# A hand-kept list scheduler gets a new order of loads, a later end and a longer wait for hosts

## The chip, the cores and the metric

One Trainium2 chip, one core of it. The kernel is one launch. Its time is the device time of that core in microseconds; lower is better. The matrix engine is TensorE (PE; its weight loads are listed as PEld), VectorE is DVE, ScalarE is ACT, GpSimd is POOL, and SyncE (SP) issues most of the transfers.

## The reference

Two branches share one normalized input. The first is a diagonal state-space layer (S4D) over 2048 tokens and 576 channels, which the reference does as a long convolution with a kernel of sums of 128 complex exponentials; the second is a two-layer perceptron with 4608 hidden units. Everything is float32.

```python
x = A_u                                   # 1 x 2048 x 576
xn = _layernorm(x)
# branch A: K[d, l] = 2 Re sum_n C[d, n] exp(A[d, n] dt[d] l), y = causal convolution of xn with K
dt = jnp.exp(log_dt)
A = -jnp.exp(log_A_real) + 1j * A_imag    # 576 x 128 poles
C = (C_real + 1j * C_imag) * dt[:, None]
P = jnp.exp((A * dt[:, None])[:, :, None] * pos[None, None, :])
K = 2.0 * jnp.einsum("dn,dnl->dl", C, P).real
y = irfft(rfft(u, 2L) * rfft(K, 2L))[:L] + u * D_skip
# branch B
g = silu(gelu(_layernorm(xn) @ w1 + b1) @ w2 + b2)
out = x + y * g
```

## The kernel before

**The perceptron is the frame.** Its products run in 48 slots. A slot takes three blocks of 128 hidden units (G = 3) and 512 tokens (TB). First come three *hidden blocks*, 14 matmuls of 512 columns each (`layer1`, L546), each followed by GELU on ACT (L578), a rounded copy `hh` on ACT (L581) and the remainder `hl = h - hh` on DVE (L584): float32 is done as sums of products of such pairs. Then comes the second layer: a transposed part for the last 128 channels (L630) and four groups of nine matmuls of 448 columns, one group for each 128 tokens (L638). After each group DVE adds the result to `acc` (L643). Four slots are "turned" and do the second layer in halves of 288 columns instead (L608, added at L615). The results of hidden blocks and of groups take turns in two PSUM banks, m0 and m1, so a new block can start only when the one two before it in the row has been read: the first hidden block of a slot needs the add of the third group of the slot before.

**The weights** arrive as `raw`, and are split the same way into a rounded part (ACT, L530) and a remainder (DVE, L527). The second layer's tile is laid out in one of two ways. A *joined* set keeps all 576 columns of a row together and is split in three pieces of 576; any other keeps 448 and 128 columns apart and is split in pieces of 448, 384 and 896. `JOINED` (L456) lists the joined sets; a set serves two slots as a rule.

**The state-space branch is fitted in between.** Before it can start, the poles' *polar form* (`params`, from L778) must be worked out: four arrays, log_A_real (buffer `kt`), C_real (`pr`), C_imag (`mg`) and A_imag (`kt` again), are each loaded by four transfers of SP in pieces of 128 bytes (L793) and turned by DVE (L800); then come square roots, arctangents and sines on ACT, and on DVE reciprocals (L820, L832) and products. A table for each 16 channels follows (`tables`), and from each table a product on PE (`kgen`, L981) that makes a piece of the convolution kernel. The convolution itself is done on PE in small tiles for chunks of 96 channels (`chunk`: L1053, L1092, L1145, and the last inverse step L1177), six chunks in all; each ends with a store to `s_s` in device memory. A group of these small matmuls between two matmuls of the frame is called a *visit* below. A table's product can `ride` in a visit of the convolution, its *host*, or make a visit alone.

**Tokens 512 to 2047 are normalized** by statistics on DVE (L383, L385), roots on ACT (L389), a reciprocal and a scaling on DVE (L393, L405); the inputs are loaded by SP (L358). Tokens of the second half go back to memory for later (`y_s`, L407).

**The order is made at build time.** `Order` is a list scheduler: *lines* of steps, each step with an engine, a planned duration, needs, and perhaps an earliest time (`at`). At each point it takes, of the lines' next steps, the one that can start earliest; between equals the line that stands first in `od.lines`. What it traces is then fixed: each engine runs its instructions in that order, and an instruction that waits holds back everything behind it on its engine. A load is a step without an engine, and its planned duration is only a guess of when the data are there:

```python
fetch = [step(None, 6.0, lambda k=k: load(k), at=t, mark=("praw", k)) for k, t in ((0, 44.0), (2, 56.0), (3, 60.0), (1, 66.0))]
```

The line `nl` holds the norms, `pl` the polar form. At the end, `ml` holds the last stores: for the last 96 channels of tokens of the first half it loads the convolution's result (L706, into `xc`), multiplies it by the gate (`gated`, L711) and adds the input (`summed`, L716). `END` (L1535) is the planned time by which the convolution's steps are spread out, and `ALONE` (L1536) is how long a table's product that is ready waits for a host before it goes alone.

Of the kernel before, what the change touches and what calls it, by code (L numbers as in the profile page):

```python
# [23 lines left out]
NCH = D // CH  # L24
# [19 lines left out]
def dve(n):  # L44
    return 0.075 + 0.00104 * n
# [163 lines left out]
def step(eng, dur, fn, need=(), mark=None, cv=0, at=0.0, late=0.0, tbl=None, by=1e9):  # L209
    return dict(eng=eng, dur=dur, fn=fn, need=tuple(need), mark=mark, cv=cv, at=at, late=late, tbl=tbl, by=by)  # L210
# [3 lines left out]
def mixer_kernel(ctx, tc, u, log_a_real, a_imag, c_real, c_imag, log_dt, d_skip, w1, b1, w2, b2,  # L214
# [19 lines left out]
    def dram(ap_of, offset, ap):  # L234
        return bass.AP(tensor=ap_of.tensor, offset=ap_of.offset + offset, ap=ap)
# [217 lines left out]
    SEQ = [(n, g, tb) for n, (g, tbs) in enumerate(SETS) for tb in tbs]  # L453
    FIRST, GATE = (0, 3, 2 * NG, 2 * NG + 1), (2 * NG - 4, 2 * NG - 1)
    TURNED = (2 * NG - 4, 2 * NG - 1, 4 * NG - 2, 4 * NG - 1)
    JOINED = {SEQ[slot][0] for slot in TURNED} | set(range(6))  # L456
    DT = D - DA
    for n, (g, _) in enumerate(SETS):
        PARTS += [(n, g, 1, i) for i in range(KB + 1)] + [(n, g, 2, i) for i in range(G)]
# [37 lines left out]
    def split_raw(low_on=nc.vector):  # L497
# [14 lines left out]
        else:  # L512
            joined, m = half in JOINED, P
            if i == 0:
# [178 lines left out]
    def combine_load(b, n, c0, c1, part=None):  # L693
        m = c1 - c0
        if part is None:
            XS[b] = [sb.tile([P, D], F32, name="row", bufs=NROW)[:, :n * m].rearrange("p (i d) -> p i d", i=n) for _ in range(3)]
        elif part == 0:
            kt = [sb.tile([P, 12, 64], F32, name="kt", bufs=2).rearrange("p a b -> p (a b)") for _ in range(2)]
            xc = sb.tile([P, 2, 32, 24], F32, name="xc", bufs=NXC).rearrange("p a b c -> p (a b c)")
            XS[b] = [t[:, :n * m].rearrange("p (i d) -> p i d", i=n) for t in (kt[0], xc, kt[1])]  # L700
        x, s, g = XS[b]
        if part != 1:
            nc.gpsimd.dma_start(x, u_s[:, b:b + n, c0:c1])
            nc.gpsimd.dma_start(g, g_s[b:b + n, :, c0:c1].rearrange("i p d -> p i d"))
        if part != 0:
            nc.gpsimd.dma_start(s, s_s[:, b:b + n, c0:c1])  # L706
# [71 lines left out]
    def params():  # L778
# [12 lines left out]
        def load(k):  # L791
            for q in range(4):
                nc.sync.dma_start(PRM[k][32 * q:32 * q + 32, :D].rearrange("p (b j) -> p b j", j=32), dram(  # L793
                    src[k], 32 * q, [[N, 32], [32 * N, D // 32], [1, 32]]))
        fetch = [step(None, 6.0, lambda k=k: load(k), at=t, mark=("praw", k)) for k, t in ((0, 44.0), (2, 56.0), (3, 60.0), (1, 66.0))]
        add(None, 12.0, lambda: nc.sync.dma_start(dt, dram(log_dt, 0, [[0, P], [1, D]])), at=24.0)
        add("ACT", act(D), lambda: nc.scalar.activation(dt, dt, AF.Exp), tbl="exp", late=0.0)
        V, A = nc.vector, nc.scalar
# [16 lines left out]
        t = T[2]  # L815
# [396 lines left out]
    od = Order(tc, nc)  # L1212
    od.pinned = True
    el, wl2, wl, nl2, pl, pl2, pl3, pl4, pl5, nl, ml, ml2, xl, wx, c3, c2, c1, kl, tl, sl, vl, gl, fl, f2l = [od.line() for _ in range(24)]
# [117 lines left out]
    def row_lines():  # L1332

        Y = [A2F[:, k:k + TB] for k in (2 * D, PT0 + 4 * D, 0, D, PT0 + 4 * D + TB, PT0 + 4 * D + 2 * TB)]
        X, T = [Y[k] for k in (0, 1, 2, 0, 3)], Y[4:]

        def store(t):
            nc.gpsimd.dma_start(dram(y4_s, t * P * D, [[D, 64], [64 * D, 2], [1, D]]), YT[4 + t])

        def load(i):  # L1340
            for q in range(4 if i < KB else 2):
                y = X[i][32 * q:32 * q + 32]
                if i < KB:
                    nc.gpsimd.dma_start(y.rearrange("p (b d) -> p b d", b=4), dram(
                        y4_s, i * P * D + P * q, [[D, 32], [32 * D, 4], [1, P]]))
                else:
                    nc.gpsimd.dma_start(y.rearrange("p (b j) -> p b j", j=32), dram(
                        y4_s, KB * P + 32 * q, [[D, 32], [32 * D, NT], [1, 32]]))

        def blocks(i):  # L1350
            x, y = T[i % 2], X[i]
            if i < KB:
                nc.vector.transpose(x.rearrange("p (k b t) -> p k b t", k=4, b=4),
                                    y.rearrange("p (b k j) -> p k b j", k=4, b=4))
            else:
                nc.vector.transpose(x[:64], y[:64])

        def places(i):
            y = T[i % 2]
            c = slice(i * P, (i + 1) * P)  # L1360
            if i < KB:
                return y.rearrange("p (k t) -> p k t", k=4), XH[:, :, 1, c], XL[:, :, 1, c]
            return y[:64], XR[:64, 1], XR[64:, 1]

        def high(i):
            y, h, _ = places(i)
            nc.scalar.activation(h, y, AF.Copy)

        def low(i):
            y, h, lo = places(i)  # L1370
            nc.vector.tensor_sub(lo, y, h.bitcast(F32))
        issue = od.line()
        for i in range(KB + 1):
            out = od.line()["steps"]
            if i < KB:
                out.append(step("POOL", 0.7, lambda i=i: store(i), need=[("yn", 4 + i)], mark=("yo", i)))
            out.append(step(None, 6.0, lambda: None, need=[("yo", min(i, 3))], mark=("ys", i)))
            issue["steps"].append(step("POOL", 2.4 if i < KB else 1.2, lambda i=i: load(i), mark=("yi", i),
                                       need=[("ys", i)] + ([("yt", 0)] if i == 3 else [])))
            od.line()["steps"].append(step(None, 5.0 if i < KB else 7.0, lambda: None, need=[("yi", i)], mark=("yl", i)))  # L1380
            a, b, c = od.line(), od.line(), od.line()
            a["steps"].append(step("DVE", dve(TB), lambda i=i: blocks(i), mark=("yt", i),
                                   need=[("yl", i)] + ([("y2", i - 2)] if i > 1 else [])))
            b["steps"].append(step("ACT", act(TB), lambda i=i: high(i), mark=("yh", i), need=[("yt", i)]))
            c["steps"].append(step("DVE", dve(TB), lambda i=i: low(i), need=[("yh", i)], mark=("y2", i) if i < KB else ("x", 1)))
        k = [i for i, x in enumerate(od.lines) if x is pl][0]
        od.lines = od.lines[-26:] + od.lines[:k] + [nl] + [x for x in od.lines[k:-26] if x is not nl]

    YB = []

# [43 lines left out]
    def weigh_in(which):  # L1434
# [3 lines left out]
        end = od.t["PE"] + sum(ln[G:] if which == 1 else ln[:G])  # L1438
        apart = which == 2 and SEQ[turn[0]][0] not in JOINED
        for i in range(m):  # L1440
# [27 lines left out]
    def w2_parts(n, j, hid):  # L1468
        if n in JOINED:
            return hid  # L1470
# [22 lines left out]
    for k in range(4):  # L1493
        gl["steps"].append(step("POOL", 5.0, lambda k=k: part.update({k: load_g2(k)}), mark=("g2", k),
                                need=[("g2c", k - 1)] if k else []))
# [24 lines left out]
    def end_line():  # L1520
        for c, c0, c1, sets in ((NCH - 3, 0, CE, [(b, 1) for b in range(8)]), (NCH - 2, CE, CL, [(0, 4), (4, 4)])):
            for b, n in sets:
                a = (b, n, c0, c1)
                ml["steps"].append(step(None, 8.0 if b else 12.0, lambda a=a: combine_load(*a), need=[("st", c), ("u", NT - 1)]))
                ml["steps"].append(step("DVE", 2 * dve(n * (c1 - c0)), lambda a=a: (gated(*a), summed(*a))))
                ml["steps"].append(step(None, 4.0, lambda: None))
        a = (0, 8, CL, D)
        ml["steps"].append(step(None, 1.0, lambda: combine_load(*a, 0), need=[("k1", NCH - 1, 1), ("x1", NCH - 1)]))
        ml["steps"].append(step(None, 11.0, lambda: combine_load(*a, 1), need=[("st", NCH - 1)]))
        ml["steps"].append(step("DVE", dve(8 * CH) + 0.1, lambda: gated(*a)))  # L1530
        ml["steps"].append(step("DVE", dve(8 * CH) + 0.1, lambda: summed(*a)))


    pace = dict(left=NCH * (2 + 2 + 4), last=0.0, started=False)
    END = 930.0  # L1535
    ALONE = 5.0  # L1536

    def pe_turns(limit=1, any_time=False, all_lines=True):
        for x in (nl, pl, ml) + ((c3, c1, kl) if all_lines else ()):
            n = 0  # L1540
            while n < (2 if x in (c1, nl) else limit):
# [3 lines left out]
                if x is c1:  # L1545
                    now = od.t["PE"]
                    gap = (END - now) / max(pace["left"], 1)
                    if n == 0 and pace["started"] and now < pace["last"] + 0.50 * gap and not any_time:
# [20 lines left out]
    later(mid - 4, G - 1, lambda: x_free(0))  # L1569
    later(mid - 1, G - 1, lambda: x_free(1))  # L1570
    later(NSLOT - 10, 4, end_line)
    sl["steps"].append(step(None, 11.0, last_s, need=[("st", NCH - 1)], mark="s8"))
    for k in range(8):
        c3["steps"].append(step(None, 5.0 if k == 0 else 2.0, lambda k=k: last_x(k), need=[("i1", NCH - 1), ("u", NT - 1)], mark=("x8", k)))

# [49 lines left out]
    for slot in range(NSLOT):  # L1625
# [4 lines left out]
        for pos in range(NPOS):  # L1630
            if pos < G:
                need = wmark(n, 1) + [("x", tb)]
# [16 lines left out]
                for k, (a, b, c) in enumerate(cell, pos + 1 - len(cell)):  # L1649
                    by = hidden_by(pos, k)  # L1650
                    if slot == NSLOT - 1 and k:
                        a = seeded(a, tb, k)
# [6 lines left out]
            else:  # L1659
# [6 lines left out]
                need = [wmark(n, 2)[i] for i in w2_parts(n, j, hid)] + [("h", slot, i) for i in hid]  # L1666
# [19 lines left out]
                if last or halves:  # L1686
                    add = cell[0]
                    dh, k = (terms[0][1], 1) if halves else (0, 2)
# [9 lines left out]
                    if final:  # L1698
                        b = 8 + 4 * tb + j
                        x, y = (el, el2) if slot < NSLOT - 1 else (od.line(),) * 2  # L1700
# [72 lines left out]
```

## Time and profile before

| | |
|---|---|
| median of three runs | 1068.91 us (1068.3 to 1071.31) |
| the profiled execution | 1070.33 us, its span 1068.2 us |
| PE busy | 1057.6 us, 99% of the span |
| DVE busy | 936.7 us, 88% |
| ACT busy | 677.4 us, 63% |
| granted TensorE clock | 0.999 |

The span runs from the first to the last instruction; 2.1 us of the execution's time lie outside it. Matmuls overlap, and their ends are modelled, so what a matmul costs is read from start to start: an undisturbed one of 512 columns is listed with 0.39 us and is followed by the next after 0.227 us.

### The profile page before, as it was taken

The numbers are of one execution on the slowest core, as the hardware profiler recorded it, in microseconds if no ns is written. First come the engines' busy times: TensorE is split into PE (matmuls) and PEld (weight loads), VectorE is DVE, ScalarE is ACT, GpSimd is POOL, SyncE is SP. The second block draws the span as 40 slices with busy tenths as digits, with TensorE's granted clock in tenths as the row PEclk, the third lists the DMA queues.
The fourth block names the chain that finished last, engine by engine and source line by source line (L and its number), as shares of the span: only waits on it lengthen the run. The fifth ranks groups of instructions, "written<-read, shape, count | busy, mean of one in ns | idle before, by whom it ended". The sixth has DMA issues, their size and how long they took to land. (4 is left out here: it accounts for less than half of the span.)

```text
span 1068.2 us, 23535 instructions
## 1 busy us (share of the span) xinstructions
PE 1057.6 (99%) x9515; PEld 874.5 (82%) x9515; DVE 936.7 (88%) x1550; ACT 677.4 (63%) x1056; POOL 212.2 (20%) x294
## 2 busy tenths in 40 slices
PE   9999999999999999999999999999999999999997
PEld 7887888888878887888878888788877888778886
DVE  7688768889999899999999999899899999957656
ACT  6567639877655767657667675666685675625344
POOL 5668743201000002000120000200002022322020
PEclk9999999999999999999999999999999999999999
DMA  7885446664223143454521315222421446465145
GB/s 230 238 259 171 121 144 224 214 163 142 62 69 91 43 100 99 120 134 116 124 83 48 110 39 121 74 75 64 96 86 45 132 118 150 125 188 162 24 126 170
DMA packets 149213, 130.93 MB, mean 123 GB/s; under 512 B 99020, under 2 KB 121072, under 8 KB 148080
## 3 DMA queue, kind: packets, MB, share of 16 engines
q1 hardware_dynamic: 132592, 79.76, 28.2%
q0 software_dynamic: 15760, 48.70, 14.9%
q8 instruction: 75, 1.23, 0.5%
q10 hardware_dynamic: 752, 0.97, 0.3%
q14 instruction: 34, 0.28, 0.1%
HBM read 98.90 MB, written 35.19 MB: 126 GB/s over the span
## 5 line engine op out<-in xcount | busy, mean ns | idle before, releaser
L638 PE MATMUL m<-w2s,hh 128*128 128x448 f32 x1056 | 301.9, 367 | 0.4 <-DVE acc L643 0.2
L638 PEld LDWEIGHTS m<-w2s,hh 128*128 128x128 f32 x1056 | 196.1, 188 | 28.9 <-issue 7.0
L578 ACT ACTIVATE h<-m,b1t 128x512 f32<-128x512 f32 x144 | 99.2, 689 | 188.2 <-PE m L546 183.6
L638 PE MATMUL m<-w2s,hl 128*128 128x448 f32 x528 | 191.5, 363 | 0.0
L546 PE MATMUL m<-XH,w1h 128*128 128x512 f32 x564 | 155.5, 398 | 0.0
L546 PE MATMUL m<-XL,w1h 128*128 128x512 f32 x564 | 151.6, 391 | 0.0
L546 PE MATMUL m<-XH,w1l 128*128 128x512 f32 x564 | 151.0, 390 | 0.0
L584 DVE TENSOR_TENSOR hl<-h,hh 128x512 fp32r<-128x512 f32 x144 | 99.1, 689 | 53.7 <-ACT hh L581 53.3
L546 PEld LDWEIGHTS m<-XH,w1h 128*128 128x128 f32 x564 | 103.4, 188 | 30.9 <-issue 9.1
L546 PEld LDWEIGHTS m<-XL,w1h 128*128 128x128 f32 x564 | 105.9, 188 | 23.0
L546 PEld LDWEIGHTS m<-XH,w1l 128*128 128x128 f32 x564 | 105.9, 188 | 22.4
L881 POOL DMA_DIRECT2D par<-par_s x36 | 27.4, 762 | 484.2 <-DVE mg L924 423.7
L643 DVE TENSOR_TENSOR acc<-m,acc 128x448 f32<-128x448 f32 x160 | 98.4, 615 | 19.0 <-PE m L638 17.7
L638 PEld LDWEIGHTS m<-w2s,hl 128*128 128x128 f32 x528 | 99.1, 188 | 7.4
L630 PE MATMUL m<-hh,w2s 128*128 128x512 f32 x264 | 98.9, 402 | 0.0
L581 ACT ACTIVATE hh<-h 128x512 fp32r<-128x512 f32 x144 | 90.6, 630 | 3.3
L530 ACT ACTIVATE w2s<-raw 128x576 fp32r<-128x576 f32 (+3 forms) x75 | 46.4, 675 | 48.6 <-PE m L638 47.0
L924 DVE TENSOR_TENSOR mg<-par 128x1024 f32<-128x1024 f32 x72 | 67.9, 952 | 0.7
L630 PEld LDWEIGHTS m<-hh,w2s 128*128 128x128 f32 x264 | 49.6, 188 | 17.5 <-issue 5.1
L527 DVE TENSOR_TENSOR w1l<-raw,w1h 128x384 fp32r<-128x384 f32 x98 | 49.8, 558 | 13.8 <-ACT w1h L530 13.7
L546 PE MATMUL m<-XR,w1r 128*128 128x512 f32 x141 | 54.9, 389 | 0.0
L546 PE MATMUL m<-XR,w1s 128*128 128x512 f32 x141 | 54.9, 389 | 0.0
(227 smaller groups left out, 1866.3 us busy)
## 6 DMA issues: line engine op xcount, KB each, us to landing
raw<-in_B_w_dram SPq DMA_DIRECT2D x75, 288.0 KB, 3.5
raw<-in_B_w_dram SPq DMA_DIRECT2D x100, 192.0 KB, 3.4
par_s<-A POOLq DMA_DIRECT2D x8, 1080.0 KB, 5.6
par<-par_s POOLq DMA_DIRECT2D x36, 240.0 KB, 3.4
f2t<-f2q SPq DMA_DIRECT2D x24, 256.0 KB, 3.8
raw<-in_B_w_dram SPq DMA_DIRECT2D x50, 96.0 KB, 3.9
u_s<-in_A_u_dram POOLq DMA_DIRECT2D x16, 288.0 KB, 4.1
xc<-xn_s SPq DMA_DIRECT2D x48, 96.0 KB, 4.1
```

The lines of the kernel that those rows point to most:

```text
L527: low_on.tensor_sub(lo, r[:m], h[:m].bitcast(F32))
L530: nc.scalar.activation(h, r, AF.Copy)
L546: nc.tensor.matmul(q, a, b, start=j == 0, stop=j == len(ops) - 1)
L578: nc.scalar.activation(t, q, AF.Gelu_apprx_tanh, bias=b1t[:, g * G + i:g * G + i + 1], scale=1.0)
L581: LAST[0] = nc.scalar.activation(hh[:, i], t, AF.Copy)
L584: nc.vector.tensor_sub(hl[:, i], t, hh[:, i].bitcast(F32))
L630: nc.tensor.matmul(q, a[:, i], b[:, i], start=first and i == 0 and k == 0, stop=slot in CONV and i == G - 1 and k == 2, skip_group_check=True)
L638: nc.tensor.matmul(q[:, :DA], a[:, i, key * P:key * P + P], b[:, i], start=i == 0 and k == 0, stop=i == G - 1 and k == 2)
L643: nc.vector.tensor_add(o, Q2.pop(key)[:, :DA], bias2[:, :DA] if first else o)
L881: nc.gpsimd.dma_start(PAR[b].rearrange("p (g i) k -> p g (i k)", g=4), dram(par_s, (b // 6 * CH + b % 6 * 4) * NPAR, [[D * NPAR, P], [24 * ...
L924: nc.vector.tensor_mul(T["m"][:, :, 64 * k:64 * k + 8 * n].rearrange("p c (i j) -> p c i j", i=n), bc(PAR[b][:, :, e8:e8 + n], 3, 8), bc(P ...
```

## The change

Five places of the scheduler's input change; no instruction's work does, apart from the layout of some weight tiles. The loads of the poles' arrays go out in the order C_real, log_A_real, C_imag, A_imag. The line of the polar form is put in front of the line of the norms. The sets 2 to 5 of the second layer's weights are no longer joined. Two planned waits near the end are longer. `END` is 30 us later, and a table's product waits 9 us instead of 5 for a host.

```diff
-    JOINED = {SEQ[slot][0] for slot in TURNED} | set(range(6))
+    JOINED = {SEQ[slot][0] for slot in TURNED} | {0, 1}
...
-        fetch = [step(None, 6.0, lambda k=k: load(k), at=t, mark=("praw", k)) for k, t in ((0, 44.0), (2, 56.0), (3, 60.0), (1, 66.0))]
+        fetch = [step(None, 6.0, lambda k=k: load(k), at=t, mark=("praw", k)) for k, t in ((2, 44.0), (0, 50.0), (3, 56.0), (1, 62.0))]
...
-        od.lines = od.lines[-26:] + od.lines[:k] + [nl] + [x for x in od.lines[k:-26] if x is not nl]
+        first = [pl, nl]
+        od.lines = od.lines[-26:] + od.lines[:k] + first + [x for x in od.lines[k:-26] if all(x is not y for y in first)]
...
-        ml["steps"].append(step(None, 11.0, lambda: combine_load(*a, 1), need=[("st", NCH - 1)]))
+        ml["steps"].append(step(None, 16.0, lambda: combine_load(*a, 1), need=[("st", NCH - 1)]))
...
-    END = 930.0
-    ALONE = 5.0
+    END = 960.0
+    ALONE = 9.0
...
-    sl["steps"].append(step(None, 11.0, last_s, need=[("st", NCH - 1)], mark="s8"))
+    sl["steps"].append(step(None, 14.0, last_s, need=[("st", NCH - 1)], mark="s8"))
```

**SP, from the fourth set of weights on.** This is SP's queue before, about 45 to 75 us into the span: `raw` are weights, `w` and `v` are the memory in which the second half's inputs (in_A_u) are put.

```order
L473 DMA raw<-in_B_w_dram 128x576
L793 DMA kt<-in_A_log_A_real_dram 32x18x32 x4
L473 DMA raw<-in_B_w_dram 128x576 x2
L475 DMA raw<-in_B_w_dram 128x384 x3
L358 DMA w<-in_A_u_dram 128x576 x6
L358 DMA v<-in_A_u_dram 128x576 x2
L475 DMA raw<-in_B_w_dram 128x384
L478 DMA raw<-in_B_w_dram 64x384 x2
L793 DMA pr<-in_A_C_real_dram 32x18x32 x4
L793 DMA mg<-in_A_C_imag_dram 32x18x32 x4
L793 DMA kt<-in_A_A_imag_dram 32x18x32 x4
```

And this is the same stretch of the changed kernel:

```order
L473 DMA raw<-in_B_w_dram 128x576
L793 DMA pr<-in_A_C_real_dram 32x18x32 x4
L473 DMA raw<-in_B_w_dram 128x576 x2
L793 DMA kt<-in_A_log_A_real_dram 32x18x32 x4
L475 DMA raw<-in_B_w_dram 128x384
L358 DMA w<-in_A_u_dram 128x576 x6
L358 DMA v<-in_A_u_dram 128x576 x2
L475 DMA raw<-in_B_w_dram 128x384 x3
L478 DMA raw<-in_B_w_dram 64x384 x2
L793 DMA mg<-in_A_C_imag_dram 32x18x32 x4
L793 DMA kt<-in_A_A_imag_dram 32x18x32 x4
```

C_real has gone from behind the inputs to the front of them, log_A_real one place back, and two of the four weight pieces behind the inputs; C_imag stands behind 25 transfers of this stretch, as before.

**DVE, in the second layer of the third slot.** The four L643 are the adds of the slot's four groups; `w` are inputs of the second half. Before:

```order
L643 TENSOR_TENSOR acc<-m_708,acc 128x448
L383 BN_STATS U<-w 128x6
L385 BN_AGGR U<-U 128x2
L1371 TENSOR_TENSOR XR<-A_83,XR 64x512
L643 TENSOR_TENSOR acc<-m_731,acc 128x448
L383 BN_STATS U<-w 128x6 x2
L385 BN_AGGR U<-U 128x2
L383 BN_STATS U<-w 128x6
L643 TENSOR_TENSOR acc<-m_746,acc 128x448
L383 BN_STATS U<-w 128x6
L385 BN_AGGR U<-U 128x2
L800 STREAM_TRANSPOSE xc<-pr 128x576
```

The same adds in the changed kernel:

```order
L643 TENSOR_TENSOR acc<-m_712,acc 128x448
L800 STREAM_TRANSPOSE xc<-pr 128x576
L1371 TENSOR_TENSOR XR<-A_83,XR 64x512
L643 TENSOR_TENSOR acc<-m_735,acc 128x448
L800 STREAM_TRANSPOSE A_83<-mg 128x576
L383 BN_STATS U<-w 128x6
L385 BN_AGGR U<-U 128x2
L643 TENSOR_TENSOR acc<-m_749,acc 128x448
L383 BN_STATS U<-w 128x6 x2
L385 BN_AGGR U<-U 128x2
L811 TENSOR_TENSOR kt<-kt,pr 128x576
L643 TENSOR_TENSOR acc<-m_764,acc 128x448
```

The turn of C_real (`pr`) has moved from behind the third add to behind the first, and the turn of C_imag (`mg`), which stood a slot later, now stands in front of the third add.

**DVE, in the last slot but one.** The L615 are the adds of the turned slot's halves, and L711 reads `xc`, the last chunk's result. Before:

```order
L615 TENSOR_TENSOR acc<-m_11398,acc 128x288
L756 SCALAR_TENSOR_TENSOR acc<-row,acc 128x576
L711 TENSOR_TENSOR xc<-xc,kt 128x768
L615 TENSOR_TENSOR acc<-m_11413,acc 128x288
L615 TENSOR_TENSOR acc<-m_11425,acc 128x288
```

In the changed kernel, from the same add (the fourth of eight) on:

```order
L615 TENSOR_TENSOR acc<-m_11391,acc 128x288
L756 SCALAR_TENSOR_TENSOR acc<-row,acc 128x576
L615 TENSOR_TENSOR acc<-m_11406,acc 128x288
L756 SCALAR_TENSOR_TENSOR acc<-row,acc 128x576
L615 TENSOR_TENSOR acc<-m_11419,acc 128x288
L615 TENSOR_TENSOR acc<-m_11432,acc 128x288
L756 SCALAR_TENSOR_TENSOR acc<-row,acc 128x576
L615 TENSOR_TENSOR acc<-m_11445,acc 128x288
L756 SCALAR_TENSOR_TENSOR acc<-row,acc 128x576
L763 TENSOR_TENSOR w<-w,acc 128x576
L767 TENSOR_TENSOR A_83<-A_83,w 128x576
L711 TENSOR_TENSOR xc<-xc,kt 128x768
```

L711 has moved behind all of the slot's adds. (One more L763 stands ahead of it, left out here.) PE's own order has as many matmuls as before. Its visits go from 80 to 75: tables' products alone from 14 to 9, and 27 instead of 22 ride. Behind the last inverse step (L1177) 200 matmuls are left instead of 214, one hidden block fewer.

## Rows read from the trace of the kernel before

**Rows 1.** The page, busy time of each engine, its share of the span, instructions.

```profile
PE 1057.6 (99%) x9515; PEld 874.5 (82%) x9515; DVE 936.7 (88%) x1550; ACT 677.4 (63%) x1056; POOL 212.2 (20%) x294
```

**Rows 2.** Waits of PE: who for whom, us in total, times, longest.

```profile
PE m L630 <- DVE hl L584: 1.3, 2, 1.0
...
PE m L638 <- DVE acc L643: 0.2, 1, 0.2
```

**Rows 3.** Timeline of PE, 82 to 84 us: start, length, instruction, idle before.

```profile
82.63 0.40 PE L630 MATMUL m<-hh,w2s 128*128 128x512 f32 x1
83.98 0.50 PE L630 MATMUL m<-hl,w2s 128*128 128x512 f32 x1 [0.95 <-DVE hl L584]
```

**Rows 4.** Timeline of PE around a table's product alone, a host alone, and both.

```profile
227.71 0.39 PE L546 MATMUL m<-XR,w1s 128*128 128x512 f32 x1
...
230.09 1.07 PE L546 MATMUL m<-XL,w1h 128*128 128x512 f32 x4
...
253.24 0.39 PE L546 MATMUL m<-XR,w1s 128*128 128x512 f32 x1
...
255.42 1.07 PE L546 MATMUL m<-XL,w1h 128*128 128x512 f32 x4
...
406.38 0.39 PE L546 MATMUL m<-XR,w1s 128*128 128x512 f32 x1
...
409.59 0.63 PE L546 MATMUL m<-XL,w1h 128*128 128x512 f32 x2
```

**Rows 5.** Timeline of PE: 27 matmuls of a joined set, a hidden block, 27 matmuls apart.

```profile
64.45 0.57 PE L638 MATMUL m<-w2s,hh 128*128 128x448 f32 x2
...
69.92 1.07 PE L546 MATMUL m<-XH,w1h 128*128 128x512 f32 x4
...
73.10 1.08 PE L546 MATMUL m<-XH,w1h 128*128 128x512 f32 x4
...
833.53 0.56 PE L638 MATMUL m<-w2s,hh 128*128 128x448 f32 x2
...
838.93 0.40 PE L546 MATMUL m<-XH,w1h 128*128 128x512 f32 x1
```

**Rows 6.** Timeline of DVE, 68 to 72 us.

```profile
68.64 0.61 DVE L643 TENSOR_TENSOR acc<-m,acc 128x448 f32<-128x448 f32 x1
...
69.65 0.21 DVE L385 BATCH_NORM_AGGREGATE U<-U 128x2 f32<-128x12 f32 x1
71.54 0.78 DVE L800 STREAM_TRANSPOSE xc<-pr 128x576 f32<-128x576 f32 x1 [1.69 <-DMA pr<-in_A_C_real_dram]
```

**Rows 7.** Timeline of SP's issues, 63 to 72 us.

```profile
63.76 5.11 SPq L793 DMA_DIRECT2D pr<-in_A_C_real_dram  x4
68.91 2.40 SPq L793 DMA_DIRECT2D mg<-in_A_C_imag_dram  x4
```

**Rows 8.** Tile mg, 60 to 90 us: its issues (ns min/median/max, first and last start) and landings.

```profile
L793 SPq DMA_DIRECT2D mg<-in_A_C_imag_dram x4: 496/496/784, 68.9 to 70.8; - x4
...
DMA to landing us min/median/max: 2.3/2.3/2.4
```

**Rows 9.** Two stretches: busy us of each engine, clock, share of DMA, GB/s.

```profile
50.00:56.00 6.00, 6.00 (x28) 5.07 (x27) 4.84 (x9) 3.73 (x5) 5.66 (x9) 1.00 0.77 237
56.00:70.00 14.00, 14.00 (x67) 12.29 (x66) 12.42 (x26) 8.70 (x14) 7.93 (x6) 1.00 0.99 308
```

**Rows 10.** Timeline of DVE: a reciprocal of the polar form, and the multiply L711.

```profile
109.33 1.94 DVE L820 RECIPROCAL pr<-pr 128x288 f32<-128x288 f32 x1
...
1040.63 0.96 DVE L711 TENSOR_TENSOR xc<-xc,kt 128x768 f32<-128x768 f32 x1 [2.36 <-DMA xc<-s_s]
```

**Rows 11.** Timeline of PE near the end.

```profile
1042.01 0.54 PE L608 MATMUL m<-w2s,hh 128*128 128x288 f32 x2 [1.34 <-DVE acc L615]
1042.38 0.29 PE L608 MATMUL m<-w2s,hl 128*128 128x288 f32 x1
...
1042.78 0.29 PE L608 MATMUL m<-w2s,hl 128*128 128x288 f32 x1
```

## The prediction

> **What bounds the kernel now.** I read the busy times of the engines first: PE works for 1057.6 of 1068.2 us [rows 1], at a granted clock of 1.00 (the last column but two of the two stretches in [rows 9], and 0.999 over the whole run in the table above). So PE is the bound, and only two things can move the time: what PE's stream costs when nothing disturbs it, and the places where it stands. For the second I took PE's waits, grouped by whom it waits for. They are few: 1.3 us in two waits for `hl` and 0.2 us in one for the add of a group [rows 2], and 1.34 in one for the add of a half [rows 11]. Each costs a little more than its listed idle time. The wait in [rows 3] lists 0.95, yet from the start before it to its own start are 1.35, and an undisturbed matmul takes 0.227 (14 of a hidden block in 73.10 - 69.92 = 3.18 [rows 5]): 1.12 are lost, 0.17 more than listed, since the matmul before it is counted as longer than its turn. And the matmul behind such a wait is late by about 0.11: in [rows 11] the two L608 behind the wait take 0.37 from start to start, where the next three take 1042.78 - 1042.38 = 0.40, or 0.27 for two. So 0.28 come to the idle time of each wait.
>
> For the stream itself I compared stretches of equal work: visits with and without a ride [rows 4], and 27 matmuls of a joined and of an unjoined set [rows 5].
>
> **Rides.** Between two matmuls of the frame, a table's product alone takes 230.09 - 227.71 = 2.38, a host alone 255.42 - 253.24 = 2.18, and both in one visit 409.59 - 406.38 = 3.21 [rows 4]. Each of these stretches also holds five undisturbed matmuls of the frame, one ahead of the small ones and four behind, 5 x 0.227 = 1.135. So the visits cost 1.245, 1.045 and 2.075, and a ride saves 1.245 + 1.045 - 2.075 = 0.215: one change between the two kinds of matmul less. Five more ride: **-1.1**. I take it for all five although hosts differ in length; the bounds are 0, if other hosts save nothing, and -1.4, with 0.06 more for the rounding of the starts.
>
> A rule of the Trainium skill (TensorE: Matmul & The Clock Gate, Part 2: What happens when you issue a matmul) says that PE loads the next weights while an earlier matmul still runs, unless the row groups conflict. By it a switch would cost nothing, and the sum below would be 1.1 higher. The rows show 0.215 for the switch, so I keep them; the rule is a rival below.
>
> **Layout of sets 2 to 5.** 27 matmuls of a joined set take 69.92 - 64.45 = 5.47, of one apart 838.93 - 833.53 = 5.40 [rows 5]. A slot has 36, and four sets serve eight slots: 8 x 36/27 x 0.07 = **-0.7**. The splitting on ACT and DVE covers the same elements, in pieces of other sizes; it lies beside PE. Bounds: 0, if the difference is one of these stretches, and -1.0.
>
> **The end.** L711 waits 2.36 for the load of `xc` [rows 10] on DVE, in front of the adds of halves that PE needs to go on, and so PE stands 1.34 [rows 11]. In the changed order L711 stands behind all adds of that slot, so what waits with it is no longer needed by a matmul of that slot. The last inverse step comes one hidden block (3.18) nearer the end, but L711 moves back by more. **-1.6** (1.34 + 0.28). What follows the last matmul stays.
>
> **The early waits of `hl` and of an add.** In the fourth slot DVE has statistics, the turn of C_imag and the first steps of an arctangent in front of two `hl` and an add. These instructions leave their places. 1.3 + 0.2 + 3 x 0.28 = **-2.3**.
>
> **The new wait.** This is the loss. The turn of C_imag (L800 of `mg`) now stands in front of the third add of the third slot, and the next slot's first hidden block needs the bank that this add reads. Before, that block started at 69.92 [rows 5]. When will C_imag be there? Its last issue started at 70.8 and it landed 2.3 later [rows 8], at 73.1, which is after the block's start. It has as many transfers ahead of it as before. Between 50 and 56 us the DMA engines are busy for 0.77 of the time, from 56 to 70 for 0.99 [rows 9]: bytes that go earlier can fill 0.23 x 6 = 1.4 us of the first stretch, no more. So C_imag lands at 71.7 if all of that is used, at 73.1 if none is. The lowest that I can give is from C_real, which is turned at 71.54 at once when it lands [rows 6]: had C_imag changed places with it wholly, and gained the 1.4 too, it would be 70.1. I take 71.7, since C_real now goes out in that emptier stretch.
>
> The rule of the Trainium skill that speaks against the new order is in DMA: Bandwidth & Descriptors, Issuing engines are not separate DMA queues: whoever issues them, all transfers run on the same 16 engines and interleave. By it alone C_imag comes when its bytes' turn comes, at 73.1, and the sum would be 1.4 higher, 1069.6. The share of 0.99 agrees; the 0.77 before it is why I don't follow it to the end.
>
> From landing to PE: 0.1 until DVE starts (an estimate), the turn 0.78, and a statistic, its aggregate and an add, which took 69.65 + 0.21 - 68.64 = 1.22 in a row [rows 6], 2.1 together. PE goes on at 71.7 + 2.1 = 73.8 instead of 69.92: 3.9, and 0.11 for the matmul behind it: **+4.0**. With 70.1 and 73.1 it is 2.4 and 5.4. Behind that L800 on DVE stand the third add itself, statistics and the fourth add; nobody but PE waits for them at once. SP's issues aren't held: they went from 63.76 to 71.31 without a gap of note [rows 7], and the loads now ahead wait for no DVE step.
>
> **What is late next.** The polar form comes earlier, ahead of the norms, and its reciprocals of 1.94 each [rows 10] now stand among the `hl` and adds of the third and fourth slots. A hidden block takes 3.18 [rows 5] and `hl` has about one such block's time, so one reciprocal is hidden; two together with an add (3.9 + 0.6) are not, by 1.3. **+1.0**, with bounds 0 (each stands behind the needed add) and 2.0 (two such places of about 1.0).
>
> **Middle of the run.** `END` moves the convolution's visits without changing their work. PE hardly waits there now, and I see no new cause: 0, bounds ±0.5.
>
> **Sum.** -1.1 - 0.7 - 1.6 - 2.3 + 4.0 + 1.0 = -0.7. The profiled execution, 1070.33, would be 1069.6; it is 1.42 above the median of the runs, 1068.91, so the median becomes **1068.2**. With the wait's and the follow-on's bounds and the middle's, the forecast's own range is 1065.1 to 1071.1.
>
> **Rivals.**
>
> *C_imag is there in time.* If it lands by 67.8 (69.92 - 2.1), nothing waits; then the follow-on mostly goes as well, since the polar form starts in the hidden part of the slot. -5.7: 1063.2. For it: 1.4 us of idle DMA, and that transfers need not finish in the order of issue. Against it: it must come 5.3 earlier than before with as many transfers ahead.
>
> *The reciprocals stand bare (slower).* Of the polar form's four reciprocals (L820, L832), all in front of what PE needs: 4 x 1.94 = 7.8 instead of 1.0, and -0.7 + 6.8 = +6.1, a median of 1075. It decides for slower from where the follow-on waits exceed 4.9 (3.2 + 0.7 + 1.0), that is with two and a half reciprocals uncovered. For it: DVE is busy for 88% of the span [rows 1], and this stretch is its fullest. Against it: in the trace of before the reciprocal at 109.33 starts right behind an add, with PE supplied.
>
> *The wait at the end only moves.* If L711's data come 3.2 later with the last inverse step and the stores behind it wait, the -1.6 is given back at the very end: 1069.8. For it: the 2.36 that it waits now. Against it: a whole turned slot's adds now lie ahead of it.
>
> *The rides don't do what they are for.* If a product costs PE as much inside a host as alone, or the longer `ALONE` makes no ride, +1.1: 1069.3. Against it: the 0.215 of [rows 4], and the order, which has 75 visits.
>
> **How the numbers follow.** The forecast has 0.57, C_imag in time 0.17, bare reciprocals 0.12, the moved wait 0.09, rides for nothing 0.05. A measurement of this kernel can tell about 0.3%, 3.2 us, from no change: 1065.7 and 1072.1. Faster is the first rival and 0.05 of the forecast's lower end, 0.22; slower is the second without its mild cases, 0.10; the rest, 0.68, is the same. The range goes from 1063.0, which takes in half of the first rival, to 1071.5, the end of the forecast's own with a little for the moved wait; 0.09 below and 0.11 above are left out.
>
> **What would show it.** Right, if DVE shows L800 of `mg` at 69 to 72 with idle time before it that a DMA ends; PE's first hidden block of the fourth slot waits there 2.4 to 5.4 for an add at L643; L638 of sets 2 to 5 goes at 0.2007 a matmul; 75 visits; no wait at L608 near 1042, and L711 behind the slot's adds. Wrong, if that block starts near 70 without a wait, if `hl` or adds of the third and fourth slots are waited for by more than 2 us in all, or if a wait of over 1 us turns up at the end or in the middle.

## The result and the profile after

The changed kernel takes 1072.34 us (median of nine runs, 1070.36 to 1074.26), the kernel before in the same measurement 1070.01 (1068.3 to 1071.31): 1.0025 of before, with an interval from 1.0016 to 1.0034. That is 2.3 us slower, and above the range of the prediction. Its profiled execution took 1073.9 with a span of 1072.1, 3.9 more than the span in the table above, so the first two traces show somewhat more than the medians do.

PE is busy for 1058.7 us, nearly as before [rows 1]. What has grown is its waiting. These are the waits of PE after, as in [rows 2] (who for whom, us in total, times, longest):

```profile
PE m L546 <- DVE acc L643: 2.7, 2, 1.4
PE m L638 <- DVE acc L643: 1.6, 3, 0.9
...
PE m L546 <- ACT h L578: 1.1, 3, 0.7
PE m L630 <- DVE hl L584: 0.7, 1, 0.7
```

The wait at L608 is gone. In its place are nine others, and six of these nine lie between 150 and 545 us, where the prediction had put nothing. Most go back to three instructions of DVE that stand ahead of their data. Here are these three (start, length, instruction, idle time before it and what ended it), each with the first add or `hl` behind it:

```profile
70.02 0.78 DVE L800 STREAM_TRANSPOSE A<-mg 128x576 f32<-128x576 f32 x1 [2.09 <-DMA mg<-in_A_C_imag_dram]
...
71.30 0.57 DVE L643 TENSOR_TENSOR acc<-m,acc 128x448 f32<-128x448 f32 x1
...
150.38 1.23 DVE L899 TENSOR_TENSOR w<-par,tv 128x1024 f32<-128x1024 f32 x1 [3.25 <-issue]
151.52 0.62 DVE L643 TENSOR_TENSOR acc<-m,acc 128x448 f32<-128x448 f32 x1
...
526.19 0.70 DVE L1404 STREAM_TRANSPOSE row<-row 64x512 f32<-64x512 f32 x1 [4.31 <-DMA row<-y_s]
...
529.08 0.69 DVE L584 TENSOR_TENSOR hl<-h,hh 128x512 fp32r<-128x512 f32 x1
```

And this is what PE does behind them:

```profile
72.02 1.16 PE L546 MATMUL m<-XH,w1h 128*128 128x512 f32 x4 [1.41 <-DVE acc L643]
...
152.19 1.20 PE L546 MATMUL m<-XH,w1h 128*128 128x512 f32 x4 [1.29 <-DVE acc L643]
...
155.95 1.20 PE L546 MATMUL m<-XH,w1h 128*128 128x512 f32 x4 [0.28 <-ACT h L578]
...
535.04 0.50 PE L630 MATMUL m<-hl,w2s 128*128 128x512 f32 x1 [0.69 <-DVE hl L584]
539.18 0.67 PE L638 MATMUL m<-w2s,hh 128*128 128x448 f32 x2 [0.94 <-DVE acc L643]
541.50 0.67 PE L638 MATMUL m<-w2s,hh 128*128 128x448 f32 x2 [0.23 <-DVE acc L643]
```

The first pair is the wait that was forecast. The second is the first step of the first table (L899), which reads `par`. POOL sends that load at 146.9, and it lands 3.4 later; DVE has nothing to do from 147.1 on but stands at L899, with an add behind it that PE needs. Before, the load left at 153.5 and L899 read it only at 167.6 (the two first tables: lengths in ns, first and last start):

```profile
L881 POOL DMA_DIRECT2D par<-par_s x2: 792/796/801, 153.5 to 179.4; - x2
L899 DVE TENSOR_TENSOR w<-par,tv x2: 1217/1221/1225, 167.6 to 182.9; 128x1024 f32<-128x1024 f32 x2
```

The third is the last piece of the second half's inputs. It is late because of SP's queue. Before, it was issued ahead of the eight loads of the convolution, and DVE turned it without idle time (the change makes the kernel one line longer: L1398 and L1403 of before are L1399 and L1404 after):

```profile
508.26 2.00 SPq L1398 DMA_DIRECT2D row<-y_s  x2
510.30 7.84 SPq L1023 DMA_DIRECT2D xc<-xn_s  x8
```

```profile
514.17 0.70 DVE L1403 STREAM_TRANSPOSE row<-row 64x512 f32<-64x512 f32 x1
```

After, it stands behind them, and eight issues that go slowly hold it for 8 us:

```profile
512.00 7.99 SPq L1023 DMA_DIRECT2D xc<-xn_s  x8
520.10 3.22 SPq L1399 DMA_DIRECT2D row<-y_s  x2
```

At the end, L711 starts without any idle time, where [rows 10] showed 2.36:

```profile
1051.43 0.95 DVE L711 TENSOR_TENSOR xc<-xc,kt 128x768 f32<-128x768 f32 x1
```

### The profile page after: what moved, and what is told of

Read it like the earlier page. It is cut to its first block, busy times and chain, and to the rows that moved or that the text cites. A ratio compares the mean times of both kernels' runs of the same rounds, so it can differ in the third digit from the quotient of the medians.

```text
span 1072.1 us, 23559 instructions
## 1 busy us (share of the span) xinstructions
PE 1058.7 (99%) x9515; PEld 873.7 (81%) x9515; DVE 934.4 (87%) x1550; ACT 693.1 (65%) x1068; POOL 207.5 (19%) x294
## 4 chain that ended last, share of the span: by engine, by line
PE 79%; DVE 10%; ACT 4%; DMA 4%; issue 2%; POOL 1%; SPq 0%; DVEq 0%; ACTq 0%
PE m L546 34%; PE m L638 24%; PE m L630 7%; PE cv L981 3%; PE cv L1092 3%; PE m L608 2%; PE cv L1053 2%; PE cv L1145 1%; DVE acc L643 1%; PE cv L1177 1%; DMA f2q<-in_f_dram 1%; ACT A L1154 1%; DMA raw<-in_B_w_dram 1%; DVE pr L1113 1%; POOL v L414 1%
## 5 line engine op out<-in xcount | busy, mean ns | idle before, releaser
L638 PE MATMUL m<-w2s,hh 128*128 128x448 f32 x1056 | 300.3, 365 | 1.7 <-DVE acc L643 1.6
L638 PEld LDWEIGHTS m<-w2s,hh 128*128 128x128 f32 x1056 | 196.6, 188 | 28.4 <-DVE acc L643 4.7
L638 PE MATMUL m<-w2s,hl 128*128 128x448 f32 x528 | 191.1, 362 | 0.0
L643 DVE TENSOR_TENSOR acc<-m,acc 128x448 f32<-128x448 f32 x160 | 98.2, 614 | 10.7 <-PE m L638 9.7
L638 PEld LDWEIGHTS m<-w2s,hl 128*128 128x128 f32 x528 | 99.0, 187 | 7.2
L530 ACT ACTIVATE w2s<-raw 128x448 fp32r<-128x448 f32 (+3 forms) x75 | 46.8, 677 | 46.5 <-PE m L638 42.0
L905 ACT ACTIVATE w<-w 128x1024 int32<-128x1024 f32 x36 | 38.0, 1056 | 51.2 <-DVE w L902 51.2
L527 DVE TENSOR_TENSOR w2s<-raw,w2s 128x448 fp32r<-128x448 f32 (+3 forms) x75 | 53.7, 748 | 4.9 <-ACT w2s L530 4.8
```

Source lines behind the costliest of these rows:

```text
L527: low_on.tensor_sub(lo, r[:m], h[:m].bitcast(F32))
L530: nc.scalar.activation(h, r, AF.Copy)
L638: nc.tensor.matmul(q[:, :DA], a[:, i, key * P:key * P + P], b[:, i], start=i == 0 and k == 0, stop=i == G - 1 and k == 2)
L643: nc.vector.tensor_add(o, Q2.pop(key)[:, :DA], bias2[:, :DA] if first else o)
L905: nc.scalar.activation(T["w"][:, 0].bitcast(I32), T["w"][:, 1], AF.Copy)
```

## The experiments

Two theories stood against each other. **A:** the loss is made of a few separate in-order waits of DVE for loads, each with one instruction that stands too early. **B:** DVE is simply too full, or one part of the change (the polar form, the layout) shifts everything, so that removing one wait only moves it. Losses of PE below count what a matmul starts later than an undisturbed one would, with the matmul behind it; that is 0.3 or less above the idle time listed.

**One load on another queue.** Everything as in the changed kernel, but the last piece of the inputs is issued by POOL.

```diff
-                nc.sync.dma_start(y[32 * q:32 * q + 32]...
+                (nc.sync if kb < KB or not tb else nc.gpsimd).dma_start(y[32 * q:32 * q + 32]...
```

> The changed kernel, with one edit: the two transfers of the last piece of y_s (L1399) are issued by POOL instead of SP, so that they no longer stand behind eight loads of the convolution. Theory A (the loss in the middle comes from an in-order wait of DVE for that load at 526 us): the idle time of 4.3 before L1404 goes, PE's waits for hl and adds between 530 and 545 (3.0 with the matmuls behind them) and the stall inside the visit at 528.7 (0.4) go too, so the time falls by 3.0 to 3.4, to 0.9994 of before. Theory B (DVE is simply too full there, and what isn't late at 526 is late a few microseconds on): at most 1 us is won, 1.0015 of before or more.

It measured 0.9997 of before (0.9988 to 1.0006), 1069.82 us. The load leaves at once, and DVE no longer waits for it:

```profile
515.08 1.33 POOL L1399 DMA_DIRECT2D row<-y_s  x2
```

```profile
520.98 0.69 DVE L1404 STREAM_TRANSPOSE row<-row 64x512 f32<-64x512 f32 x1
```

No wait of PE is left between 500 and 620. Theory A holds for this one: 0.0028 won is 3.0 us, uncertain by about 1.4, since each of the two ratios is known to 0.0009.

**The first table's load planned longer.**

```diff
-        return ([step(None, 6.0 if b < 3 else 4.5, lambda: load_par(b), ...
+        return ([step(None, 10.0 if b == 0 else 6.0 if b < 3 else 4.5, lambda: load_par(b), ...
```

> The changed kernel, with the planned duration of the first load of par 10 us instead of 6, which puts L899 behind the add that PE waits for at 152 us. Theory A (each loss is an instruction of DVE that stands ahead of its data): PE's waits at 152 and 156 go, -1.5 to -2.1, about 1.0006 of before. Theory B (the tables then come later and the wait only moves to the next slot, where the first tables are turned into products): within 0.5 of the changed kernel, 1.0021 to 1.0027 of before.

It measured 1.0000 (0.9992 to 1.0009), also 1069.82 us. L899 now stands behind the fourth add; it still waits, but nothing that PE needs is held by it:

```profile
147.65 0.62 DVE L643 TENSOR_TENSOR acc<-m,acc 128x448 f32<-128x448 f32 x1 [0.60 <-PE m L638]
149.88 1.23 DVE L899 TENSOR_TENSOR w<-par,tv 128x1024 f32<-128x1024 f32 x1 [1.61 <-DMA par<-par_s]
```

The waits at 152 and 156 are gone, and so are those of 0.2 to 0.6 at 247 and 250 (the one at 272 stays, 0.13). In the changed kernel a turn of the convolution (L1040), which waited 1.34 for ACT, and a table's product (L935) had stood among the adds there; here other steps do. Theory A again: 1.9 for the first pair, and 0.8 that it hadn't counted.

**`ALONE` back at 5.**

```diff
-    ALONE = 9.0
+    ALONE = 5.0
```

> The changed kernel with ALONE back at 5: 77 visits instead of 75, and the last piece of y_s is loaded ahead of the convolution's loads. Theory A (the longer ALONE moved the load behind the others and made the loss in the middle): -3.4 for the waits of 530 to 545, +0.4 for two rides less, 0.9997 of before. Theory B (the layout of sets 2 to 5 or the polar form made it): the waits between 520 and 545 stay, +0.4 for the rides, 1.003 of before.

It measured 1.0111 (1.0098 to 1.0124), 1081.66 us. Neither theory expected that. The stretch from 520 to 545 has no wait of PE, as theory A had it. But a new one came near the end:

```profile
1039.44 2.07 PE L546 MATMUL m<-XH,w1h 128*128 128x512 f32 x4 [8.13 <-ACT h L578]
```

**The polar form's edits alone**, on the kernel before: the order of the four loads, and the line in front of the norms.

> The kernel before with only the loads' order and the polar form's line changed; 79 visits. Theory A (the polar form's edits pay 2.3 for the early waits and cost 1.65 at 72, 0.9 at 58 and 2.0 at 152 to 156; the middle isn't touched): +2.0 to +2.5, 1.002 of before. Theory B (the whole loss comes from the polar form, which shifts all tables): the middle's waits are there as well, +5 or more, 1.005 of before.

It measured 1.0133 (1.0117 to 1.0148), 1084.34 us, and neither theory had that either. The waits between 150 and 250 are there (1.5 at 152 with what follows; theory A had counted two of them), so they come from the polar form's edits. Those between 530 and 545, which theory B expected, are not. And the same wait near the end is. In this trace one sees where it comes from. First SP's queue, then ACT, then PE, then stretches (us busy of PE, PEld, DVE, ACT and POOL, granted clock, DMA share, GB/s):

```profile
1021.95 10.65 SPq L663 DMA_DIRECT2D acc<-bias  x16
1034.05 0.33 SPq L665 DMA_DIRECT2D bias<-in_B_b_dram  x1
1034.43 0.42 SPq L473 DMA_DIRECT2D raw<-in_B_w_dram  x1
```

```profile
1039.17 0.68 ACT L530 ACTIVATE w2s<-raw 128x576 fp32r<-128x576 f32 x1 [11.88 <-DMA raw<-in_B_w_dram]
1039.76 0.67 ACT L578 ACTIVATE h<-m,b1t 128x512 f32<-128x512 f32 x1
```

```profile
1028.00:1032.00 4.00, 4.00 (x20) 3.28 (x18) 0.18 (x1) 0.00 (x0) 0.00 (x0) 1.00 0.36 84
1032.00:1040.00 8.00, 0.36 (x2) 0.00 (x0) 0.11 (x1) 0.82 (x2) 0.00 (x0) 0.80 0.50 144
1040.00:1044.00 4.00, 3.51 (x9) 2.81 (x10) 2.03 (x3) 2.27 (x4) 0.00 (x0) 0.55 0.01 2
```

The last weight piece stands behind sixteen loads of the start value for `acc`, whose issue takes 10.65 us. ACT waits for that piece in front of a GELU, the GELU frees a bank, and PE stands for 8.1. With `ALONE` at 5 in the changed kernel it was the same piece: it left at 1033.42, behind sixteen such loads, and ACT waited 11.91 for it. In the changed kernel itself all three weight pieces stand ahead of the sixteen loads:

```profile
1018.83 1.73 SPq L473 DMA_DIRECT2D raw<-in_B_w_dram  x3
1022.40 11.18 SPq L663 DMA_DIRECT2D acc<-bias  x16
```

So the parts of the change don't add up. The polar form's edits bring a stall of 8 us near the end; the longer `ALONE` takes it away, and brings the wait at 526. In the run before this one `END` and the layout had their new values, and `ALONE` alone decided which of the two stalls there was.

**Both repairs.**

> The changed kernel with both repairs: the last piece of y_s issued by POOL, and the first load of par planned with 10 us. Theory A (the two losses are separate waits of DVE): the two gains add, 0.9972 to 0.9976 of before. Theory B (what the one repair wins, the other would have won as well, since both only give DVE room): 0.9995 to 1.0000, as with either alone.

It measured 0.9970 (0.9958 to 0.9982), 1066.55 us. The gains add, as theory A says; the only wait of DVE's making over 0.2 that is left is the one for C_imag:

```profile
PE m L546 <- DVE acc L643: 1.4, 1, 1.4
```

**C_imag turned later as well.**

```diff
-        turns = lambda k, to: add("DVE", d, ..., need=..., at=48.0)
+        turns = lambda k, to: add("DVE", d, ..., need=..., at=70.0 if k == 3 else 48.0)
```

> As the last, and the turn of C_imag may start in the plan only at 70 us, which puts it behind the third and fourth add of the third slot. Theory A (the wait at 71 is only that of the add for C_imag): another -1.4 to -1.7, 0.9957 to 0.9962 of before. Theory B (a later polar form puts its steps in front of hl, as in the kernel before): waits for hl of 1.0 to 2.3 between 75 and 110 take the gain back, 0.997 to 0.999.

It measured 0.9968 (0.9956 to 0.9980), which can't be told from the last run. The wait at 71 is gone (1.5 with what follows), and two others stand in this trace: one for `h` at 58 (1.1) and one for `hl` at 122 (0.8, the polar form's steps stand ahead of it). The first lies ahead of the moved turn and differs from trace to trace, up to 1.2, so it isn't this edit's doing; the second is of theory B's kind, though later and smaller than it said.

**The layout undone.** The changed kernel with `JOINED` as before.

> The changed kernel with sets 2 to 5 joined again; visits and loads stand as in the changed kernel. By the term of the prediction (27 matmuls 5.47 instead of 5.40 in eight slots) +0.7, 1.0031 of before. Theory B (the layout costs PE nothing; it changes only the pieces in which ACT and DVE split): 1.0020 to 1.0027, and 27 matmuls of these sets take the same time in both traces.

It measured 1.0040 (1.0027 to 1.0054). The interval holds the expected 1.0031 and overlaps that of the changed kernel, so the time alone settles nothing; the trace does. 27 matmuls of such a set, up to the next hidden block, in the changed kernel (142.12 to 147.52, 5.40) and in this one (142.45 to 147.96, 5.51, which is 0.04 above the usual: of the other seven slots of these sets six go at 0.2027 or 0.2028 a matmul, or 5.47):

```profile
142.12 0.56 PE L638 MATMUL m<-w2s,hh 128*128 128x448 f32 x2
...
147.52 0.87 PE L546 MATMUL m<-XH,w1h 128*128 128x512 f32 x3
```

```profile
142.45 0.57 PE L638 MATMUL m<-w2s,hh 128*128 128x448 f32 x2
...
147.96 1.09 PE L546 MATMUL m<-XH,w1h 128*128 128x512 f32 x4
```

**The two planned waits alone**, on the kernel before.

> The kernel before with only the two planned waits at the end longer (16 and 14). By the term of the prediction: L711 goes behind all adds of its slot, PE's wait of 1.34 at 1042 goes, -1.6, 0.9985 of before. Theory B (the last stores wait for L711 instead): the time after the last matmul grows by as much, 1.0000 of before.

It measured 0.9972 (0.9962 to 0.9982), 1067.06 us: more than the expected 1.6. L711 starts behind the adds, without idle time, and the time from PE's last start to the end is the same 5.8 as before. The median fell by 2.4; against the second trace of before, below, the span fell by the expected 1.6, and no trace shows where the other 0.8 comes from. But its trace holds a surprise: up to the last slots its instructions are those of the kernel before, and the waits for `hl` of [rows 2] aren't there. So the next run was a second look at the kernel before.

> The kernel before once more, for a second trace. Theory A (the two waits for hl at 81 and 84 follow from DVE's order): they stand in this trace too, 1.3 idle. Theory B (they depend on when loads happened to land in that one execution, since the run with only the two planned waits has the same instructions there and none of the waits): under 0.3 here, and a span 1 to 2 us shorter than the first.

The span was 1065.9, the time 1068.02 us. PE waits for no `hl`, and DVE does this, to be laid beside [rows 6]:

```profile
69.00 0.21 DVE L385 BATCH_NORM_AGGREGATE U<-U 128x2 f32<-128x12 f32 x1
69.19 0.78 DVE L800 STREAM_TRANSPOSE xc<-pr 128x576 f32<-128x576 f32 x1
```

In the first trace L800 stood for 1.69 until C_real landed; here the data are there, since SP began the issues of C_real at 61.51 instead of 63.76 [rows 7]. DVE runs 2.35 earlier from that point on, PE only 0.6, and that is what `hl` lacked at 81 and 84. Theory B: the waits for `hl` of [rows 2] and [rows 3] were those of one execution.

> The changed kernel once more. Theory A (its waits at 71, 152, 247 to 272 and 530 to 542 follow from the order): all stand here with the same length within 0.4, as they did in the runs that didn't touch them. The wait for h at 58 is 0.1 to 1.2 in the runs so far and may be any of these.

The span was 1068.8, the time 1070.57 us. The waits at 72, 152, 156, 247, 250 and 272 stand there with lengths as before, the largest difference being 0.24. The wait for the inputs' last piece is shorter, and PE lost only 0.4 to it instead of 3.0:

```profile
DVE w L899 <- issue: 3.5, 1, 3.5
DVE A L800 <- DMA mg<-in_A_C_imag_dram: 2.2, 1, 2.2
DVE row L1404 <- DMA row<-y_s: 1.4, 1, 1.4
```

Theory A holds but for that one: here the load left at 518.81, not 520.10, its second issue took 0.8 us instead of 2.7, and DVE stood 1.4 instead of 4.3. In the two other traces with this order on SP, those of the longer planned load and of the layout undone, DVE stood 4.1 and 5.1, and PE lost about as much as in the first.

**The loads a little later.** As the run with the later turn of C_imag, with C_real and log_A_real planned at 47 and 52, which puts them behind the three weight pieces.

> The changed kernel with the two repairs, the later turn of C_imag, and the loads of C_real and log_A_real planned 3 and 2 us later, so that C_real goes out behind the three weight pieces that ACT waits for at 54. Theory A (that wait of ACT makes PE's wait at 58): the 0.2 to 1.2 there go, -0.5, 0.9963 to 0.9968 of before. Theory B (the turned order shifts the waits only; hl at 121 and others stay): 0.9968 to 0.9975.

It measured 0.9967 (0.9954 to 0.9980). The wait at 58 isn't in this trace, as theory A says, but it was missing in the second trace of the changed kernel too, so one trace doesn't show it; and `hl` is waited for at 83 (1.0) and 122 (0.8): theory B for the time. Four versions now stand between 0.9967 and 0.9972, and no interval separates them. The simplest of them is the kernel before with the two planned waits.

## Why the prediction was wrong

Term by term, with what PE lost in each stretch, summed from its starts in the two traces of before and after each:

| term | predicted | first traces | second traces |
|---|---|---|---|
| rides | -1.1 | -1.1 | -0.9 |
| layout of sets 2 to 5 | -0.7 | -0.7 | -0.7 |
| the wait at L608 near the end | -1.6 | -1.5 | -1.8 |
| 14 to 140 us: early waits, C_imag, follow-on | -2.3 + 4.0 + 1.0 = +2.7 | 2.05 to 2.39: +0.3 | 0.42 to 1.97: +1.6 |
| 140 to 300 us | 0 | +2.9 | +3.1 |
| 500 to 545 us | 0 | +3.0 | +0.4 |

The sums are +2.9 and +1.7. The changed kernel's traces have six and five waits more, each with a late matmul of 0.11 behind it: +0.7 and +0.6. PE's last start moved by +3.9 and +2.9; 0.3 and 0.6 remain in places too small to name.

**Rides.** Right. Summed over all visits, from the matmul of the frame ahead to the one behind less one turn, they cost 128.29 before (80 visits) and 128.17 after (75), of which 0.4 is a stall inside one at 529; so 0.5 less, and five late matmuls of 0.11 less. A product alone costs 1.12, a host of 16 matmuls 0.92 and both in one visit 1.95, in all of the nine and eight such visits: 0.09 a ride, and the late matmul. The Trainium skill (TensorE: Matmul & The Clock Gate, Part 2: What happens when you issue a matmul) says that weight loads are pulled ahead of running matmuls where the row groups don't conflict or the background buffer takes them. A switch that this hid wholly would cost nothing; here it cost the 0.2.

**Layout.** Right: 5.40 against 5.51 in the run with the sets joined, and in the slots without waits a mean spacing of L638 of 0.2002 to 0.2007 after where it was 0.2027 or 0.2028 before.

**The end.** Right: PE's wait is gone after, and in the run that made this edit alone. Only the two planned waits were needed for it.

**The new wait.** Right in its place and its cause, too large in its price: 1.4 idle and 1.6 with what follows, instead of 4.0. The 2.1 from landing to PE held: C_imag landed at 69.9, and PE went on at 72.02. Of the 2.4 too many, 1.8 are the landing and 0.5 that PE came to this block at 70.45 instead of 69.92. "So C_imag lands at 71.7 if all of that is used" took as its base a landing at 73.1, which was late in that execution. In the second trace of before, C_imag's last issue is at 68.7 and it lands at 71.3. From there to 69.9 are 1.4, as much as the idle DMA time of the sum, and the share between 50 and 56 rose from 0.77 [rows 9] to 1.08; that the one comes from the other wasn't tested. The Trainium skill's rule that all issuers' transfers share the same 16 engines (DMA: Bandwidth & Descriptors, Issuing engines are not separate DMA queues) had argued for no gain at all; at 0.77 the engines were shared, but not full.

**What is late next.** The +1.0 didn't come: no wait of PE over 0.15 stands between 75 and 150 us in either trace after. What the sum lacked there is the wait for `h` at 58, 0.8 in the first trace.

**The early waits.** This step failed: "These instructions leave their places. 1.3 + 0.2 + 3 x 0.28 = -2.3." The two waits for `hl`, nearly all of it, weren't the order's alone but needed C_real's late landing in one execution [rows 6]; two other traces with the same order there have none. In the second trace the whole stretch lost 0.42, so there was next to nothing to win. This error and that of the new wait have one root, SP's queue 2 us late in the one trace that was read, and opposite signs; that they half hid each other was luck.

**The middle of the run.** This is the step that made the forecast wrong: "PE hardly waits there now, and I see no new cause: 0, bounds ±0.5." It measured +6 in the first traces and +3.4 in the second. Both main causes stood in the new order: L899 ahead of an add with its load just sent, which the polar form's edits bring by themselves, and the inputs' last piece behind eight loads on SP, which came with the longer `ALONE`. The order was read where the terms already were, and `END` and `ALONE` were taken to move only PE's visits, when every engine and queue is traced in the order that they lead to. Moving the one load to POOL and planning the other longer won 3.0 and 2.7 us (with the small waits at 247 and 250), and both together 5.9, which settles it.

What stays open: why the same wait for the inputs costs 3.0 in one execution and 0.4 in another, beyond that the load left 1.3 earlier and landed sooner. `END` wasn't tried by itself at all, and layout and `ALONE` not on the kernel before.

## What to carry to other kernels

When a list scheduler's input changes, compare the new order over the whole program on every in-order engine and queue, and look for two things: an instruction that waits for a load and has moved ahead of one that the bound engine needs, and a load that has moved behind a row of slow issues. Price such a wait from more than one execution, since a landing that one trace shows can come 2 us earlier in the next, as C_real's did here. And test edits of a scheduler one by one and left out one by one: here two numbers won 2.4 us alone, and two others, the polar form's, lost 14 alone and still stalled PE for 8 within the change until `ALONE` was longer.

## What was not expected of the hardware

While PE stood for 8.1 us its granted clock fell (0.80 over the 8 us), and in the next 4 us it was 0.55, a mixture of its two levels (1.2 and 2.4 GHz): six matmuls of 512 columns took 0.41 to 0.43 from start to start instead of 0.227 in the run with the polar form's edits alone, and nine took 0.43 in the run with `ALONE` at 5. That made the 8.1 us into losses of 9.8 and 10.6. The waits of up to 2.0 us elsewhere left the next matmuls at their 0.227, but for one that was 0.11 late.

Also, a load's place behind slow issues on SP cost more than its own transfer. Eight loads of 96 KB took 8 us to issue, sixteen of the start values 10.7, and what stood behind them left later by that. Why these issues are slow the runs don't show: the DMA share was 0.91 during the eight and 0.51 during the sixteen (in the run with the polar form's edits alone). The Trainium skill (DMA: Bandwidth & Descriptors, Issuing engines are not separate DMA queues) says that issuing from several engines saves only the sequencer's time, "which is usually small relative to the DMA itself". Here what it saved was not small: two transfers that POOL issued while SP was at its eight landed within 4.5 us of their issue, and 3.0 us were won.
